# Loading z half as bf16, denser score pairs, w2 turned by DMA and z of batch 1 moved up in a fused attention and max-out kernel

## The chip, the cores and the metric

The kernel runs on one core of one Trainium2 chip. The metric is device time in microseconds (us) of that core. Before the change it was 969.01 us (median of 3 runs, 968.8 to 970.68). The span of a profile is about 2.4 us shorter than the time (966.4 against 968.82 for the same execution).

Names: PE is TensorE, PEld its weight loads, DVE VectorE, ACT ScalarE, POOL GpSimd, SP SyncE. L147 is a line of the kernel; the changed kernel has other line numbers. A "mirror" is a 512 KB block of scores turned by DMA, because the score matrix is symmetric. "Turned" means transposed: zT is z turned, zd the cast copy of z that is turned. A transfer has landed when all its data is there. The tile a_sb holds squared scores, r_sb the relus before them, h_sb the sums copied out of the accumulators at the end of a group (the drain copy). The granted clock is the clock of TensorE in the profile, 1.00 being full; the page is the printed summary of a profile.

## The reference, cut to what matters

```python
def _attn_ref(u, v, z):                       # 8 x 3072 x 256, z 8 x 3072 x 64
    scores = (1.0 / S) * np.matmul(z, z.transpose(0, 2, 1))
    attn = np.maximum(scores, 0.0) ** 2
    return u * np.matmul(attn, v)

def _moe_ref(x, w1, w2, w_out):               # x: 24576 x 256, Dff = 1024
    return np.maximum(x @ w1, x @ w2) @ w_out
```

The kernel uses max(h1, h2) = relu(x(w1-w2)) + x w2, so it needs w15 = w1-w2 and W2o = w2 @ w_out once, and W2o needs w2 transposed (w2T).

## The kernel before

A batch has 24 tiles of 128 rows in 6 groups of 4 tiles. Groups are numbered i over all batches: i = 0 to 5 are batch 0. "Tile n of group g" below is the n-th of the 24 steps of that group. While PE multiplies the squared scores of group i with v, score pairs for later use are put in at chosen slots:

```python
    def pair_slots(i):
        if i == 0:
            return [1, 3] + list(range(6, 40, 4))
        if i == 1:
            return list(range(3, 41, 4))
        ...
    # in score_pair: two products z.zT into PSUM, then
        for h in range(2):
            s, o = s_ps[h][:, lo[h] :], r[:, h, lo[h] :]
            if h == dve_half:                       # VectorE takes one half of every third early pair
                nc.vector.tensor_single_scalar(out=o, in_=s, scalar=0.0, op=ALU.max)
            else:
                nc.scalar.activation(o, s, AF.Relu)
        ...
            nc.vector.tensor_mul(a[:, k : k + 2, :], r, r)
    ...
            early = done < 22                       # dve_half=1 if early and done % 3 == 0
```

The opening loads z of batch 0 in three pieces on SP, v on GpSimd's queue; the third piece is cast on GpSimd:

```python
        z32a = first_z(0, 4)
        z32b = first_z(4, 8)
        z32c = first_z(12, 12)
        ...
        load_v(0, 0, G)
        make_identity(nc, ident)
        for g in range(1, NG):
            load_v(0, g * G, G)
        ...
        on_pool = (nc.gpsimd.tensor_copy, nc.gpsimd.tensor_copy)
        for c in range(0, 12, 4):
            double_first(z32c, 12 + c, 4, at=c, copies=on_pool)
```

In group 2, w2 is turned on PE; at its end W2o is made ahead of the first feed-forward product (ff1, inside ff). All DMA transposes (mirrors, u, z of batch 1) go through the SP queue in program order:

```python
                if i == 2 and n == 16:
                    nc.vector.tensor_sub(w15_sb, w1_sb, w2_sb)
                    for dc in range(KD):
                        tp = mm_psum.tile([P, KF, P], bf16, name="tpw", tag="mm")
                        for j in range(KF):
                            nc.tensor.transpose(tp[:, j, :], w2_sb[:, dc, ts(j, P)], ident)
                        nc.scalar.copy(w2T_sb[:, dc, :, :], tp)
                if b + 1 < B:
                    late = int(b == 0)
                    if (g, n) == (2, 10 if b else 20):
                        load_z(b + 1, 0, NT, held=late)
                    if (g, n) == (3, 4):
                        double_z(b + 1, 0, NT)
                        zT_dma(b + 1)
    ...
            if i == 2:
                for dc in range(KD):
                    ps = mm_psum.tile([P, D], fp32, name="w2o_ps", tag="mm")
                    for nb in range(KF):
                        nc.tensor.matmul(ps, w2T_sb[:, dc, nb, :], w_out_sb[:, nb, :], ...)
                    nc.scalar.copy(W2o_sb[:, dc, :], ps)
            now = waiting if ff_follows(i) else []
            g_sbs = [ff(w) for w in now[:1]]
```

## Time and profile before

| what | value | where it is read |
|---|---|---|
| time, span | 969.01 us, 966.4 us | runs, head of the page |
| PE busy | 99% of the span | busy table |
| PE on the chain that ended last | 96% | chain of waits |
| PE idle in the first 60 us | 60 - 54.97 = 5.0 us | busy time by window |
| PE waits after 60 us | one of 0.2 us | waits of PE by window |

The head, the busy table and the chain's shares, from the page of the kernel before:

```profile
span 966.4 us, 19478 instructions
...
PE 954.8 (99%) x7994; PEld 621.6 (64%) x8042; DVE 487.2 (50%) x847; ACT 557.6 (58%) x1058; POOL 61.0 (6%) x118
...
PE 96%; DVE 1%; issue 1%; ACT 1%; DMA 1%; DVEq 0%; POOLq 0%
```

PE is the limit. So a change can win only where PE waits, or where it does work that can go. This is the view of waits, PE alone, first 60 us, kernel before. Columns: who waited, for whom; us in total, times, longest:

```profile
PE acc_134 L374 <- DVE warm L351: 1.2, 1, 1.2
PE acc_427 L199 <- DVE a_sb L166: 1.1, 3, 0.5
PE acc_427 L199 <- DVE h_sb L214: 0.5, 1, 0.5
PE s_ps L147 <- DVE r_sb L158: 0.5, 1, 0.5
PE acc_134 L199 <- DMA v_sb<-in_v_dram: 0.4, 1, 0.4
PE s_ps L147 <- ACT zT L105: 0.4, 1, 0.4
PE acc_637 L199 <- DVE a_sb L166: 0.4, 1, 0.4
PE tpz L101 <- ACT zd L88: 0.3, 1, 0.3
```

The first is the start and stays. The rest, 3.6 us by these lines, is what the opening had to give. The PE transposes of w2 and the products that read them, from the timeline of PE (start, length):

```profile
46.71 1.07 PE L439 MATMUL tpw<-ident,w_132 128*128 128x128 bf16 x16
...
52.03 1.92 PE L458 MATMUL w2o_ps<-w_out_sb,w2T 128*128 128x256 bf16 x16
```

The transposes are 1.07 us of PE.

### The profile page before, as it was taken

What the parts mean: (1) busy time and instruction counts of PE and PEld (TensorE: products, weight loads), DVE (VectorE), ACT (ScalarE), POOL (GpSimd) and SP (SyncE); (2) the same over time, 40 slices, a digit from 0 to 9 for tenths busy, and PEclk for the clock granted to TensorE, in tenths of its full rate; (3) what the DMA queues carried; (4) which work ended last, traced back from release to release, by engine and by line L of the source; (5) the groups of instructions that cost most, each with busy time, mean ns of one, the idle gap of its engine ahead of it and who ended that gap; (6) DMA issues with size and microseconds to landing.
All of it is one profiled execution on the core that took longest, in us unless ns stands there. A gap on an engine that the chain in (4) does not pass through costs nothing.

```text
span 966.4 us, 19478 instructions
## 1 busy us (share of the span) xinstructions
PE 954.8 (99%) x7994; PEld 621.6 (64%) x8042; DVE 487.2 (50%) x847; ACT 557.6 (58%) x1058; POOL 61.0 (6%) x118
## 2 busy tenths in 40 slices
PE   8999999999999999999999999999999999999998
PEld 4465667675666756667566765676756776566655
DVE  6746454463555534555346553464545554445433
ACT  6757466563575645756456564565556656466433
POOL 3001000100000000000000000000000000000000
PEclk9999999999999999999999999999999999999999
DMA  9999798988689976999869988699967998767611
GB/s 186 186 207 175 135 156 158 179 149 166 134 140 188 146 157 126 164 185 148 150 133 146 184 152 160 131 162 176 150 141 140 157 170 168 135 131 145 124 56 44
DMA packets 382296, 145.99 MB, mean 151 GB/s; under 512 B 360832, under 2 KB 361984, under 8 KB 382208
## 3 DMA queue, kind: packets, MB, share of 16 engines
q1 hardware_dynamic: 365792, 115.25, 62.5%
q0 software_dynamic: 16416, 29.50, 20.8%
q8 instruction: 63, 1.03, 0.4%
q14 instruction: 25, 0.20, 0.1%
HBM read 59.77 MB, written 25.17 MB: 88 GB/s over the span
## 4 chain that ended last, share of the span: by engine, by line
PE 96%; DVE 1%; issue 1%; ACT 1%; DMA 1%; DVEq 0%; POOLq 0%
PE o_ps L263 17%; PE d_ps L234 17%; PE s_ps L147 7%; PE o_ps L255 4%; DMA v_sb<-in_v_dram 1%; DVE a_sb L166 1%; PE acc_12604 L199 1%; PE acc_6354 L199 1%; PE acc_4771 L199 1%; PE acc_3187 L199 1%; PE acc_11103 L199 1%; PE acc_9519 L199 1%; PE acc_7936 L199 1%; PE acc_1582 L199 1%; PE acc_1581 L199 1%
## 5 line engine op out<-in xcount | busy, mean ns | idle before, releaser
L199 PEld LDWEIGHTS <-v_sb 64*128 64x128 bf16 x4608 | 314.6, 94 | 181.4 <-issue 5.9
L160 ACT ACTIVATE r_sb<-s_ps 128x512 bf16<-128x512 f32 (+3 forms) x664 | 333.8, 555 | 90.4 <-PE s_ps L147 88.8
L166 DVE TENSOR_TENSOR a_sb<-r_sb 128x1024 bf16<-128x1024 bf16 x251 | 173.6, 692 | 243.0 <-ACT r_sb L160 239.0
L244 DVE TENSOR_SCALAR g_sb<-d_ps 128x512 bf16<-128x512 f32 x192 | 132.8, 692 | 146.1 <-PE d_ps L234 146.1
L263 PE MATMUL o_ps<-w_out_sb,g_sb 128*128 128x256 bf16 x1536 | 199.1, 273 | 0.0
L234 PE MATMUL d_ps<-xT,w_sb 128*128 128x512 bf16 x720 | 167.4, 379 | 2.6 <-issue 0.2
L263 PEld LDWEIGHTS <-g_sb 128*128 128x128 bf16 x1536 | 150.2, 98 | 20.8
L242 ACT ACTIVATE g_sb<-d_ps 128x512 bf16<-128x512 f32 x192 | 114.8, 598 | 82.0 <-PE d_ps L234 57.1
L147 PE MATMUL s_ps<-zT 64*128 64x512 bf16 (+3 forms) x672 | 148.6, 357 | 0.9 <-DVE r_sb L158 0.5
L270 ACT COPY o_sb<-o_ps 128x512 f32<-128x512 f32 x96 | 56.3, 586 | 150.3 <-PE o_ps L263 149.2
L234 PEld LDWEIGHTS <-w_sb 128*128 128x128 bf16 x768 | 73.2, 98 | 89.6 <-issue 9.8
L255 PE MATMUL o_ps<-W2o_sb,xT 128*128 128x256 bf16 x384 | 73.3, 273 | 0.0
L118 POOL DMA_DIRECT2D un<-in_u_dram x48 | 25.7, 537 | 731.2 <-DMA uT<-un 717.6
L147 PEld LDWEIGHTS <-zT 64*128 64x128 bf16 x672 | 47.6, 94 | 29.0 <-issue 4.6
L220 DVE SCALAR_TENSOR_TENSOR xT<-h_sb,uT 128x512 bf16<-128x512 f32 x96 | 61.8, 685 | 0.0
L164 DVE TENSOR_TENSOR a_sb<-r_sb 128x512 bf16<-128x512 bf16 (+3 forms) x170 | 47.9, 323 | 14.7 <-ACT r_sb L160 14.5
L255 PEld LDWEIGHTS <-xT 128*128 128x128 bf16 x384 | 37.6, 98 | 14.1
L114 POOL DMA_DIRECT2D v_sb<-in_v_dram x48 | 25.8, 546 | 59.1 <-DVE v_sb L113 58.3
L199 PE MATMUL acc_134<-a_sb,v_sb 64*128 64x512 bf16 x24 | 8.7, 377 | 0.5 <-DMA v_sb<-in_v_dram 0.4
L199 PE MATMUL acc_136<-a_sb,v_sb 64*128 64x512 bf16 x24 | 8.7, 378 | 0.0
L199 PE MATMUL acc_137<-a_sb,v_sb 64*128 64x512 bf16 x24 | 8.5, 376 | 0.0
L199 PE MATMUL acc_135<-a_sb,v_sb 64*128 64x512 bf16 x24 | 8.5, 376 | 0.0
(577 smaller groups left out, 1665.3 us busy)
## 6 DMA issues: line engine op xcount, KB each, us to landing
out_dram<-o_sb SPq DMA_DIRECT2D x47, 512.0 KB, 4.0
v_sb<-in_v_dram POOLq DMA_DIRECT2D x48, 256.0 KB, 7.0
un<-in_u_dram POOLq DMA_DIRECT2D x48, 256.0 KB, 5.0
zn<-in_z_dram POOLq DMA_DIRECT2D x7, 384.0 KB, 6.7
a_sb<-a_sb SPq DMA_TRANSPOSE x126, 2.7
at_sb<-a_sb SPq DMA_TRANSPOSE x120, 5.0
uT<-un SPq DMA_TRANSPOSE x48, 3.3
w_132<-in_moe_w_dram POOLq DMA_DIRECT2D x1, 512.0 KB, 5.1
```

What stands on the lines that cost most here:

```text
L147: nc.tensor.matmul(s_ps[h][:, lo[h] :], zT[b][rows, 2 * m + h, :], zT[b][rows, g * G + lo[h] // P : g * G + G, :].rearrange("p t c -> p (t ...
L160: nc.scalar.activation(o, s, AF.Relu)
L164: nc.vector.tensor_mul(a[:, k + h, lo[h] :], o, o)
L166: nc.vector.tensor_mul(a[:, k : k + 2, :], r, r)
L199: nc.tensor.matmul(o, v_sb[b][rows, t, ts(dc, P)], mv, start=first, stop=last)
L220: nc.vector.scalar_tensor_tensor(out=xT[:, dc, :].rearrange("p (t r) -> p t r", r=P), in0=hs[dc].rearrange("p (t r) -> p t r", r=P), scala ...
L234: nc.tensor.matmul(d_ps, w15_sb[:, kc, ts(nb, P)], xT[:, kc, :], start=(kc == 0), stop=(kc == KD - 1),)
L242: nc.scalar.activation(g_sb[:, nb, :], d_ps, AF.Relu)
L244: nc.vector.tensor_single_scalar(out=g_sb[:, nb, :], in_=d_ps, scalar=0.0, op=ALU.max)
L255: nc.tensor.matmul(o_ps[:, t, :], xT[:, dc, ts(t0 + t, P)], W2o_sb[:, dc, :], start=(dc == 0), stop=False,)
L263: nc.tensor.matmul(o_ps[:, t, :], g_sb[:, nb, ts(t0 + t, P)], w_out_sb[:, nb, :], start=False, stop=(nb == KF - 1),)
L270: nc.scalar.copy(o_sb[:, t0 : t0 + 2, :], o_ps)
```

## The change

It removes waits and work from the opening: half of z moves behind the first v tile, so that v lands sooner; score pairs come earlier and VectorE takes fewer relus; w2 is turned by DMA instead of PE; z of batch 1 is loaded and turned earlier; the last two tiles leave one by one. The diff, cut to its core:

```diff
-        for t0 in range(0, G, 2):
-            o_ps = mm_psum.tile([P, 2, D], fp32, name="o_ps", tag="mm")
+        for t0, k in ((0, 2), (2, 1), (3, 1)) if last else ((0, 2), (2, 2)):
+            o_ps = mm_psum.tile([P, k, D], fp32, name="o_ps", tag="mm")
 ... (eviction and store of k tiles instead of 2)
         if i == 0:
-            return [1, 3] + list(range(6, 40, 4))
+            return [1, 3, 6, 9, 12, 15, 18, 21, 25, 29, 33, 37]
         if i == 1:
-            return list(range(3, 41, 4))
+            return list(range(2, 40, 4))
 ...
-            early = done < 22
+            early = done < 18
 ...
-        z32c = first_z(12, 12)
 ...
-        for g in range(1, NG):
+        zn[0] = znat.tile([P, NT, dqk], bf16, name="zn")
+        nc.gpsimd.dma_start(out=zn[0][:, 12:, :], in_=by_tile(z[0])[:, 12:, :])
+        load_v(0, G, G)
+        for g in range(2, NG):
             load_v(0, g * G, G)
 ...
-        on_pool = (nc.gpsimd.tensor_copy, nc.gpsimd.tensor_copy)
-        for c in range(0, 12, 4):
-            double_first(z32c, 12 + c, 4, at=c, copies=on_pool)
+        double_first(zn[0], 12, 4, at=12, copies=[nc.gpsimd.tensor_copy] * 2)
 ...
+                if i == 0 and slot in (4, 12):
+                    both = (nc.gpsimd.tensor_copy, nc.vector.tensor_copy)
+                    lo = 16 if slot == 4 else 20
+                    double_first(zn[0], lo, 4, at=lo, copies=both)
 ...
+                if i == 1 and n == 20:
+                    nc.sync.dma_start_transpose(
+                        w2T_sb.rearrange("p c j r -> p (c j) r"),
+                        w2_sb.rearrange("p c f -> p (c f)"),
+                    )
                 if i == 2 and n == 16:
                     nc.vector.tensor_sub(w15_sb, w1_sb, w2_sb)
-                    for dc in range(KD): ... nc.tensor.transpose(...) ... nc.scalar.copy(...)
                 if b + 1 < B:
                     late = int(b == 0)
-                    if (g, n) == (2, 10 if b else 20):
+                    if (g, n) == (2, 10):
                         load_z(b + 1, 0, NT, held=late)
-                    if (g, n) == (3, 4):
+                    if (g, n) == (3, 4 if b else 0):
                         double_z(b + 1, 0, NT)
                         zT_dma(b + 1)
```

## The prediction

> **What bounds it.** TensorE. The page's busy table gives PE 99% of the 966.4 us span, the chain of waits PE 96%, granted clock 1.000. PE's waits, listed by window, are one of 0.2 us in all after 52 us. So what can be won lies in the opening and the tail. Summed by windows, PE is idle 5.0 us of the first 60, 1.2 of it the start. The waits: first product for v (landed 6.0 us after issue) 0.43; score pair for ACT's zT copy 0.39; zd cast 0.35; first accumulator for VectorE's drain copy 0.54; group 1 (31 to 37 us) for VectorE relus and squares 0.48+0.21+0.55+0.31; before w2o, a square behind the 1.22 us weight subtraction and ACT's w2T copies, 0.38.
>
> **What changes.**
> 1. 384 KB of z leave the queue that competes with the first v tile, so v lands about 1 us earlier or more. The squares (ready about 6.9) then set the first product: gain 0.4 us, 0.6 if the middle z also lands earlier. GpSimd casts fall from 6 (0.55 each) to 4, VectorE gets 2 (about 0.25 each). The Trainium skill, "DMA: Bandwidth & Descriptors", section "SWDGE vs HWDGE vs iDMA", says that a cast during DMA goes from GpSimd only; so this load stands ahead of the later v tiles, which have slack in the trace.
> 2. Denser pairs put pair 6 two slots after the zT transposes instead of four. ACT must first do seven relus at about 0.54 and the 1.02 us copy, and one cast stands behind a square on VectorE. Waits there should grow to about 1 us and eat step 1's 0.4; in exchange one score pair more is done when group 0 ends.
> 3. VectorE relu only for the first 18 pairs removes two 0.68 us relus exactly at the group 1 waits; with one pair of lead (1.08 us of PE) the 1.55 us nearly vanishes: gain 1.4. No pair stands at the end of group 0, so the 0.54 drain wait goes: gain 0.5.
> 4. w2 by DMA: 16 PE transposes leave (1.07 us, timeline), with ACT's 1.93 us of copies and most of the 0.38 wait: gain 1.4. But it becomes the third 512 KB transpose on an SP queue where those before it took 6.4 and 3.2 us to issue, and landing takes 4.3 to 10.4. Estimated landing 48 us, its reader now at 49 to 50: a wait of 0 to 2 us, mean 0.4.
> 5. Tail: the last eviction halves (0.59 to 0.37 us), as does the last store (its data moved for 0.7 us): gain 0.5.
> 6. z of batch 1 earlier: PE never waited for it, gain 0.
>
> Sum: about 0.2+1.4+0.5+1.4+0.5-0.4 = 3.6 us, all on PE's chain: from 969.0 to 965.4 us, range 963.6 to 967.9. Chances: faster 0.005, within 2% 0.985, slower 0.01.
>
> **Right or wrong in the profile.** First product at about 6.8 us (was 7.3); a PE wait for zd or zT between 10 and 12.5; none for h_sb at the first group boundary; under 0.3 us for a_sb and r_sb in group 1; no tpw lines; w2o at 48.5 to 49.5 (was 52.0); 0.5 us less after the last matmul.
>
> **What would make it wrong.** The bf16 z landing after 9 us: VectorE is in order, its cast would block squares. The w2T transpose landing late. ACT, 1.09 us per pair against PE's 1.08, limiting group 1. The run spread (968.8 to 970.7) is half the gain.

## The result, and the profile after

The changed kernel took 971.1 us (median of 5, 970.23 to 974.93), the kernel before 968.8 us in the same rounds. The ratio is 1.0026, 95% interval 1.0004 to 1.0048: slightly slower, where 3.6 us faster was predicted. Here and below a ratio is the mean time of one kernel's fast runs over that of the other's of the same rounds, so it is not quite the ratio of the medians quoted. All runs quoted here counted as fast.

The head, the busy table and the chain's shares, page of the changed kernel:

```profile
span 968.7 us, 19445 instructions
...
PE 955.2 (99%) x7978; PEld 623.1 (64%) x8026; DVE 485.5 (50%) x847; ACT 556.8 (57%) x1059; POOL 60.6 (6%) x117
...
PE 96%; DMA 2%; DVE 1%; ACT 1%; issue 0%; SPq 0%
```

PE's busy total hardly moved and its share is still 99%. These averages do not show the fault; only the DMA share of the chain rose. The waits of PE in the first 70 us of the changed kernel do show it:

```profile
PE w2o_ps L461 <- DMA w2T<-w: 4.4, 1, 4.4
PE acc L377 <- DVE warm L351: 1.2, 1, 1.2
PE s_ps L147 <- ACT zT L105: 0.6, 1, 0.6
PE acc L199 <- DVE h_sb L214: 0.4, 1, 0.4
PE s_ps L147 <- DVE zT L105: 0.3, 1, 0.3
```

All waits of PE for squares, for VectorE's relu and for v are gone: the opening worked. One new wait of 4.42 us stands above it. The w2o products were free to start at 53.55 - 4.42 = 49.1 us instead of 52.03, so 2.9 us had been won by then. They started at 53.55. The view of the tile w2T, changed kernel (for the products: nanoseconds min/median/max of one):

```profile
...
L461 PE MATMUL w2o_ps<-w_out_sb,w2T x16: 283/421/422, 53.6 to 56.7; 128*128 128x256 bf16 x16
L440 SPq DMA_TRANSPOSE w2T<-w x1: 6248/6248/6248, 45.2 to 45.2; - x1
...
  PE w2o_ps L461: 4.4, 1
...
DMA to landing us min/median/max: 8.4/8.4/8.4
```

The transpose was issued at 45.15 us and landed 8.4 us later. And the products that had waited took 421 ns each, where they took 272 before. The busy time by windows, below, tells why. The timeline of PE has it in one line (start, length, the wait before it):

```profile
53.55 3.46 PE L461 MATMUL w2o_ps<-w_out_sb,w2T 128*128 128x256 bf16 x16 [4.42 <-DMA w2T<-w]
```

Columns of the windows: window, its length, busy us (instructions) of PE, PEld, DVE, ACT, POOL, then the granted clock, the DMA share and GB/s:

```profile
49.00:50.00 1.00, 0.13 (x2) 0.00 (x0) 0.32 (x1) 0.00 (x0) 0.00 (x0) 1.00 0.97 158
...
53.00:54.00 1.00, 0.45 (x3) 0.33 (x4) 0.00 (x0) 0.00 (x0) 0.00 (x0) 0.66 1.13 214
54.00:55.00 1.00, 1.00 (x6) 0.72 (x5) 0.00 (x0) 0.00 (x0) 0.00 (x0) 0.50 1.12 201
...
56.00:57.00 1.00, 1.00 (x7) 0.69 (x6) 0.00 (x0) 0.00 (x0) 0.00 (x0) 0.63 1.17 218
57.00:58.00 1.00, 0.95 (x6) 0.46 (x5) 0.09 (x1) 0.89 (x2) 0.00 (x0) 1.00 1.12 209
```

After the idle the granted clock is 0.50, back to 1.00 by 57 us. So w2o took 3.46 us instead of 1.92. The wait and the half clock together cost 4.42 + 1.54 = 6.0 us, more than everything the change won.

The tail, by contrast, went as planned. The last piece of the chain (start, length), kernel before and then changed kernel:

```profile
962.45 0.59 ACT o_sb L270
```

```profile
965.29 0.37 ACT o_sb L271
```

From its start to the end of the span it was 966.4 - 962.45 = 3.95 us, and is 968.7 - 965.29 = 3.41 us.

### The profile page after: what moved, and what is told of

Its sections match the earlier page's. It is cut to its first block, busy times and chain, and to the rows that moved or that the text cites. A ratio compares the mean times of both kernels' runs of the same rounds, so it can differ in the third digit from the quotient of the medians.

```text
span 968.7 us, 19445 instructions
## 1 busy us (share of the span) xinstructions
PE 955.2 (99%) x7978; PEld 623.1 (64%) x8026; DVE 485.5 (50%) x847; ACT 556.8 (57%) x1059; POOL 60.6 (6%) x117
## 4 chain that ended last, share of the span: by engine, by line
PE 96%; DMA 2%; DVE 1%; ACT 1%; issue 0%; SPq 0%
PE acc L199 49%; PE o_ps L264 17%; PE d_ps L234 17%; PE s_ps L147 7%; PE o_ps L256 4%; DMA at_sb<-a_sb 1%; DMA w2T<-w 1%; ACT r_sb L160 0%; PE w2o_ps L461 0%; PE acc L377 0%; DVE a_sb L166 0%; ACT zT L105 0%; PE tpz L101 0%; DVE h_sb L417 0%; DVE r_sb L158 0%
## 5 line engine op out<-in xcount | busy, mean ns | idle before, releaser
L160 ACT ACTIVATE r_sb<-s_ps 128x512 bf16<-128x512 f32 (+3 forms) x666 | 334.6, 555 | 88.7 <-PE s_ps L147 86.9
L199 PE MATMUL acc<-a_sb,v_sb 64*128 64x512 bf16 x2688 | 340.9, 376 | 0.1
L199 PE MATMUL acc<-at_sb,v_sb 64*128 64x512 bf16 x1920 | 238.0, 376 | 0.7 <-DVE h_sb L214 0.4
L271 ACT COPY o_sb<-o_ps 128x512 f32<-128x512 f32 (+1 forms) x97 | 56.3, 581 | 150.0 <-PE o_ps L264 148.9
L205 ACT COPY h_sb<-acc 128x512 f32<-128x512 f32 x92 | 51.5, 589 | 76.2 <-PE acc L199 76.2
L207 DVE TENSOR_TENSOR h_sb<-h_sb,acc 128x512 f32<-128x512 f32 x92 | 61.1, 685 | 64.1 <-ACT h_sb L205 64.1
```

The source lines that it names most:

```text
L199: nc.tensor.matmul(o, v_sb[b][rows, t, ts(dc, P)], mv, start=first, stop=last)
L207: nc.vector.tensor_add(hs[dc], hs[dc], acc[0, dc])
L271: nc.scalar.copy(o_sb[:, t0 : t0 + k, :], o_ps)
```

## The experiments

Theory A: the whole loss is the wait of w2o for the w2T transpose and the half clock after it; the rest of the change wins what was predicted. Its rivals: B, the other parts cost something too; C, the transpose is late because the z load of batch 1 was moved into the same stretch; D, the DMA queue is full for so long that an extra transpose is paid for wherever it stands. C and D say why A's wait is so long. The kernel before gave medians of 969.29, 969.03, 968.94 and 968.88 us. Times (us), ratio to before and interval:

| run | edit | median (range) | ratio, 95% interval |
|---|---|---|---|
| changed kernel | | 971.1 (970.23 to 974.93) | 1.0026 [1.0004, 1.0048] |
| e_pe | changed, w2 on PE | 966.28 (965.56 to 966.88) | 0.9964 [0.9951, 0.9977] |
| e_early | changed, w2T queued earlier | 973.1 (966.49 to 975.12) | 1.0022 [0.9997, 1.0047] |
| e_zlate | changed, z load and turn late | 974.24 (970.93 to 980.98) | 1.0052 [1.0024, 1.008] |
| e_dummy | changed, PE kept busy in the wait | 969.74 (968.87 to 972.88) | 1.0003 [0.9985, 1.0021] |
| p_w2dma | before, w2 by DMA | 968.89 (967.69 to 971.51) | 0.9992 [0.9972, 1.0013] |
| e_pe_spare | e_pe and an unread transpose | 966.91 (965.86 to 967.21) | 0.9967 [0.9948, 0.9986] |
| e_deadline | changed, queue in order of need | 967.23 (965.02 to 970.05) | 0.9973 [0.9947, 0.9999] |
| p_pairs | before, denser pairs | 966.42 (966.22 to 970.25) | 0.9971 [0.9949, 0.9992] |
| e_zmid | changed, z load late only | 969.74 (966.35 to 972.31) | 1.0002 [0.998, 1.0023] |
| e_w2o_after_ff1 | changed, reader later | 968.77 (966.59 to 969.76) | 0.9989 [0.9975, 1.0003] |
| e_zmid_ff1 | both | 967.93 (966.86 to 973.4) | 0.9996 [0.9976, 1.0017] |
| p_zload | before, opening load | 968.45 (967.9 to 977.63) | 1.0018 [0.9986, 1.0049] |
| e_pe_zmid | e_pe, z load late | 966.04 (965.74 to 972.4) | 0.9981 [0.9962, 0.9999] |
| e_pe_zlate | e_pe, z load and turn late | 965.75 (965.61 to 966.05) | 0.9968 [0.9956, 0.998] |
| e_pe_oldload | e_pe, old opening load | 965.92 (965.8 to 966.62) | 0.9971 [0.9958, 0.9984] |
| p_tail | before, tail only | 967.94 (967.36 to 968.87) | 0.999 [0.9978, 1.0002] |

All gave correct results. Ranges are those of the fast runs listed with each kernel, five or six.

### e_pe: w2 turned on PE again

```diff
-                if i == 1 and n == 20:
-                    nc.sync.dma_start_transpose(w2T_sb..., w2_sb...)
                 if i == 2 and n == 16:
                     nc.vector.tensor_sub(w15_sb, w1_sb, w2_sb)
+                    (the PE transposes and ACT copies of the kernel before)
```

> The changed kernel with w2 turned on TensorE again, all else as changed. Theory A (the loss is the 4.42 us wait of w2o for the w2T transpose plus the half clock after it, 3.46 us for w2o where it was 1.92): both go, 1.1 us of transposes and up to 0.4 of a wait for squares come back, so 971.1 - 6.0 + 1.3 = about 966.4 us, faster than before by about 2.4. Rival B (the denser pairs or the moved z loads cost what the trace of the one run does not show): stays above 968.8.

Measured 966.28 us, within 0.2 us of theory A and below before by more than the interval. Its w2o started at 49.50 us at full clock, and no wait of PE stands in its trace after 60 us:

```profile
49.50 1.92 PE L463 MATMUL w2o_ps<-w_out_sb,w2T 128*128 128x256 bf16 x16
```

B falls: what is left of the change wins about what was predicted for it, and the DMA transpose of w2 turned a gain of 0.36% into a loss of 0.26%.

### e_dummy: PE kept busy during the wait

```diff
                     ps = mm_psum.tile([P, D], fp32, name="w2o_ps", tag="mm")
+                    for _ in range(40 if dc == 0 else 0):
+                        nc.tensor.matmul(ps, warm[:, :P], warm[:, :D], start=True, stop=True)
```

> The changed kernel with 40 products of 128x256 on a constant tile before w2o (about 4.4 us of work in place of the 4.42 us of idle; the results are overwritten). Theory A: the half clock (0.50 in the records from 53.6 to 56.7 us) comes from the idle; kept busy, the clock stays at 1.00, w2o takes 1.9 us, and the time falls by 1.5 us to about 969.6 although the wait itself is no shorter. Rival: the slow w2o comes from the DMA traffic at that time or is read wrongly; then nothing changes, about 971.

Measured 969.74 us; the span fell from 968.7 to 967.3. The windows of this run:

```profile
53.00:54.00 1.00, 1.00 (x11) 0.89 (x10) 0.00 (x0) 0.00 (x0) 0.00 (x0) 1.00 1.13 213
54.00:55.00 1.00, 1.00 (x12) 0.89 (x11) 0.00 (x0) 0.24 (x1) 0.00 (x0) 1.00 1.14 208
```

The DMA share is the same as in the changed kernel (1.13, 1.14 against 1.13, 1.12), the clock is 1.00, and the products took 272 ns (median). So the half clock came from the idle, not from the DMA traffic, and it is worth about 1.4 us. The Trainium skill, "TensorE: Matmul & The Clock Gate", section "What's actually happening", says that PE falls to half rate after an idle window of about 3.4 us; here the wait was 4.42 us, and the half rate lasted 3.4 us (53.3 to 56.7 us, read from windows of 0.2 us of the changed kernel).

### e_early: the transpose six tiles sooner

```diff
-                if i == 1 and n == 20:
+                if i == 1 and n == 14:
                     nc.sync.dma_start_transpose(w2T_sb..., w2_sb...)
```

> The changed kernel with the w2T transpose queued at tile 14 of group 1 instead of tile 20, so ahead of two mirror transposes on the SP queue. Theory A with the queue place as the reason for lateness: issued at about 34.5 us instead of 45.2, landed by about 43, no wait of w2o, clock 1.00 throughout, about 965.1 us. If the transpose were late because of what stands before it on the data side (w2 itself landing late), w2o would still wait and the time stay near 971.

The transpose was issued at 33.7 us, landed 9.6 us later, and w2o found it there at 48.6 us: that half of the expectation held. The time did not: 973.1 us, from 966.49 to 975.12. Waits of PE after 80 us in its profiled run (969.94 us, one of the faster ones):

```profile
PE s_ps L147 <- DMA zT<-zd: 3.8, 2, 2.3
PE acc L199 <- DMA at_sb<-a_sb: 0.9, 1, 0.9
```

Two transposes that stand behind it were late instead: first zT of batch 1, then a mirror. This is what D says. In the changed kernel they stand behind it too, but there PE had already lost 6.0 us and did not wait for them. The four runs above 972 us have a mean granted clock of 0.996, the profiled one 1.000, so this profile does not show all that they lost.

### e_zlate: z of batch 1 at its old places

```diff
-                    if (g, n) == (2, 10):
+                    if (g, n) == (2, 10 if b else 20):
                         load_z(b + 1, 0, NT, held=late)
-                    if (g, n) == (3, 4 if b else 0):
+                    if (g, n) == (3, 4):
```

> The changed kernel with z of batch 1 loaded and turned at its old places (tile 20 of group 2, tile 4 of group 3). Rival theory C: the transpose took 8.4 us from issue to landing because the 384 KB of z were loaded (44.3 us) into the same stretch; then it lands about 2 to 3 us sooner, the wait falls to about 2 us, and the time to about 968.5. Theory A (its place third on the queue, with mirrors taking the engines anyway): lands within 1 us of before, time 970 to 971.

w2T landed in 4.3 us instead of 8.4 and w2o had no wait worth naming (0.4 us for its first weights): C holds for the late landing, even more than expected. But the time rose to 974.24 us. Waits of PE after 60 us:

```profile
PE s_ps L147 <- DMA zT<-zd: 4.6, 1, 4.6
```

Its granted clock was again 0.50 after this idle. So with the extra transpose on the queue z could not stay at both its late places, and its move was itself what delayed that transpose. This profile (972.82 us) is one of the faster runs; those of 975 to 981 us, at a mean clock of 0.993 to 0.995, were not profiled.

### p_w2dma: the DMA transpose alone, on the kernel before

Edit: on the kernel before, the PE transposes and copies are taken out and the transpose at tile 20 of group 1 is put in, as in the diff of the change.

> The kernel before with one part of the change: w2 turned by DMA at tile 20 of group 1, z of batch 1 left at its old late place. Theory D (the DMA engines are full from 25 to 100 us, so one more 512 KB transpose is paid by whichever transfer has the next deadline): w2o finds w2T in time (landing about 49 us, as 4.3 us did in the run with the late z), but the transpose of z for batch 1 lands too late and the score pairs of batch 1 wait 3 to 5 us: time 970 to 974, slower than before. Rival C (only the collision of w2T with the moved z load costs): no wait anywhere, 969 - 1.4 = 967.6 us.

Median 968.89 us, between the two expectations: no loss, but not the 1.4 us that PE no longer spent either. The transpose landed in 5.0 us and w2o did not wait: it started at 51.4 us (52.0 before), although the first product came 0.37 us later than before. In the profiled run (its slowest, 971.51) PE then waited 3.6 us for a mirror, until 90.8 us, and not for zT. D holds in kind, not in place or size. The median is 1.3 us above the 967.6 expected without a wait; what the faster runs waited for was not profiled.

### e_zmid: only the load of z back

```diff
-                    if (g, n) == (2, 10):
+                    if (g, n) == (2, 10 if b else 20):
```

> The changed kernel with only the load of z for batch 1 put back to tile 20 of group 2; its cast and transpose stay at the changed, earlier place (tile 0 of group 3). The two runs before told two things apart only together: with load and transpose both late, the transpose of w2 landed in 4.3 us instead of 8.4, but zT came 4.6 us too late. If the collision of the two loads is the cause of the 4.42 us wait: w2T lands in 4 to 6 us, w2o waits under 0.6 us at full clock, and zT is queued at about 72 us with a wait of 0 to 2 us: 965.3 to 967.5 us. If the collision was chance: w2T lands after 8 us again and the time is 970 or more.

Timelines of the SP queue and of GpSimd, changed kernel, around the transpose (start, and time to issue):

```profile
36.03 9.02 SPq L181 DMA_TRANSPOSE at_sb<-a_sb  x2
45.15 6.25 SPq L440 DMA_TRANSPOSE w2T<-w  x1
```

```profile
44.28 0.53 POOL L75 DMA_DIRECT2D zn<-in_z_dram  x1 [10.95 <-DVE zn L74]
44.80 0.54 POOL L118 DMA_DIRECT2D un<-in_u_dram  x1
```

And the same two of e_zmid:

```profile
34.69 9.28 SPq L181 DMA_TRANSPOSE at_sb<-a_sb  x2
44.07 2.52 SPq L440 DMA_TRANSPOSE w2T<-w  x1
```

```profile
49.01 0.54 POOL L75 DMA_DIRECT2D zn<-in_z_dram  x1 [15.98 <-DVE zn L74]
49.53 0.54 POOL L118 DMA_DIRECT2D un<-in_u_dram  x1
```

The two transposes before it together took 9.0 us to issue in one and 9.3 us in the other, so the place in the queue is the same. With the 384 KB of z and the 256 KB of u queued just before it, w2T took 6.25 us to issue and 8.4 to land; without them 2.52 and 4.5:

```profile
DMA to landing us min/median/max: 4.5/4.5/4.5
```

The load of u moved along because it stands behind z in the order of GpSimd, so the share of each is not told apart. Every run that has the transpose at tile 20 and the early load agrees (8.1 to 9.5 us: e_dummy 8.2, e_w2o_after_ff1 8.1, e_pe_spare 9.5), every run with the late load too (4.3 to 5.0). C is settled: the collision is the larger part of the wait (0.6 us of it stayed in e_zmid, as a wait for the first weights). The Trainium skill, "DMA: Bandwidth & Descriptors", section "Issuing engines are not separate DMA queues", says that transfers of all issuing engines run on the same 16 DMA engines and interleave. The trace agrees: loads issued by GpSimd more than doubled the 2.52 us that a transpose on SP took to issue.

The time, however, came in two levels: 966.35, 966.45, 967.92 and 971.55, 971.71, 972.31 us. The profiled run is the fastest, and even it has this wait of PE after 60 us:

```profile
PE acc L199 <- DMA at_sb<-a_sb: 1.5, 1, 1.5
```

The three high runs were not profiled, but their mean granted clock is 0.996 to 0.998, against 1.000 in the three low ones and 0.998 in the profiled run of the changed kernel with its one stretch of half clock. So a stretch of half clock is likely in them; which transfer was late is not shown.

### e_w2o_after_ff1 and e_zmid_ff1: the reader later

```diff
-            if i == 2: (w2o products)
             now = waiting if ff_follows(i) else []
             g_sbs = [ff(w) for w in now[:1]]
+            if i == 2: (w2o products)
```

> The changed kernel with the w2o products put after the first ff1 (which does not need them), so 3.4 us later in TensorE's order; all transfers as changed. If the wait is nothing but the late landing (53.5 us against a reader at 49.1): the reader is ready at 52.5, waits about 1 us, and after so short an idle the clock should stay higher: 971.1 - 3.4 - 0.8 to 1.5 = 966.2 to 966.9 us, with perhaps up to 1 us of it given to a new wait for zT or a mirror. If the transfers only follow the reader (a queue that fills up with TensorE's progress), the wait stays near 4 us and so does the time.

> Both of the two edits above together. Expected: no wait of w2o at all, no half clock; 965.0 to 966.5 us unless zT or a mirror is waited for. This is the candidate for a version that beats both kernels with the DMA transpose kept; to beat the version with w2 turned on TensorE (966.3) it must stay under 966.

In e_w2o_after_ff1 w2T landed at 44.4 + 8.1 = 52.5 us and the reader started at 52.49 with hardly a wait (0.6 us for its first weights, none that the view lists for PE), so the queue did not merely follow the reader. The time fell less than expected, to 968.77 us: PE then waited 0.35 us for the copy of W2o, which the edit had moved closer to its use, and 2.1 us for a mirror, until 87.3 us, and the clock was 0.50 after that. e_zmid_ff1, with both edits, had no wait for w2T, and a median of 967.93 us with single runs up to 973.4 (that one profiled: waits of 2.6 us for a mirror and 2.2 us for zT). Neither beats e_pe.

### e_pe_spare: the same transpose, read by nobody

```diff
+                if i == 1 and n == 20:
+                    spare = tpool.tile([P, KD, KF, P], bf16, name="spare", tag="at_sb")
+                    nc.sync.dma_start_transpose(spare..., w2_sb...)
                 (w2T made on PE as in e_pe)
```

> The changed kernel with w2 turned on TensorE, and still the same DMA transpose of w2 at the same place, into a spare tile that nobody reads. Theory D: even without a reader it delays the transfers behind it, so waits for zT or for mirrored blocks of 1 to 4 us appear after 60 us and the time is 967.5 to 970 (against 966.3 without it). Rival (only the dependency of w2o on the transpose costs): 966.3, no new wait.

966.91 us against 966.28, in different calls; the ratios to before are 0.9967 and 0.9964. The expectation of D was too high. (The spare tile also takes one of the 13 buffers of the mirrors; the run does not separate that from the transfer.) Only a wait of 0.44 us for a mirror appeared, ending at 86.1 us. Set beside e_zmid, whose only late wait was 1.52 us and ended at 85.8 us: the difference, 1.08 us, is the 1.07 us of PE transposes that e_zmid saves. e_pe, without the extra transpose, reached the same product at about 85 us and did not wait. In these two runs the mirror came at about 86 us whatever PE did before, so what PE wins by leaving the transposes to the DMA it gives back there. In the other profiled runs with the extra transpose that waited for a mirror after 60 us it came at 86.9 to 90.8 us. So D is best put like this: with the extra 512 KB on the queue, PE can meet a late mirror at 86 us or after. This is a reading of single profiles; no run tests it by itself.

### e_deadline: transfers in the order in which they are needed

Edit: w2T at tile 14 of group 1; z of batch 1 loaded at tile 2 and turned at tile 18 of group 2; the mirrors of block 5 (needed last) held back until tile 20.

> The changed kernel with its transfers put in order of deadline: w2T queued at tile 14 of group 1, z of batch 1 loaded at tile 2 of group 2 and its transpose queued at tile 18, the mirrors of block 5 held back behind it. Theory D with slack to spend (the engines are at 0.3 to 0.8 busy from 100 to 115 us): no wait of w2o, zT or mirrors, time about 965, a little under the 966.3 with w2 turned on TensorE. If the total load and not the order is what binds, some wait of 1 to 4 us remains and the time is 967 to 970.

Three runs at 965.02 to 966.02, three at 968.43 to 970.05. In the profiled run (968.43, the fastest of the upper three) w2T took 15.4 us to land, with waits of 0.5 us for w2T, 1.4 us for VectorE's g_sb and 1.4 us for zT. The 965 of the good runs is the lowest time seen, but the kernel does not hold it.

### p_pairs, p_zload, p_tail: the other parts alone

Edits: on the kernel before, only the slots and `early = done < 18`; only the opening's loads and casts; only the tail (each as in the diff of the change).

> The kernel before with the denser score pairs and the VectorE relu for 18 pairs only, nothing else. My prediction put 1.4 us (group 1) and 0.5 us (drain) on this part: about 967.1. If the opening load is needed for it (zT not ready for pair 6, so the wait of about 1 us comes without the earlier v): about 968.

> The kernel before with only the opening's loads and casts changed (12 tiles of z as bf16 behind the first v, casts on GpSimd and VectorE). My prediction gave step 1 a gain of 0.4 to 0.6 us: v no longer waited for, first product at about 6.7 instead of 7.3 us, time 968.4 to 968.8 against 969.0 to 969.3 of before. If the opening is bound by ACT's evacuations (the copy of zT ready at about 12.8 us in either kernel) the gain at the start is gone by the score pair that waits for zT: time as before, within 0.2.

> The kernel before with only the last two tiles evicted and stored one by one. My prediction: the time from the last product to the end falls by 0.5 us (4.0 us before), so 968.4 to 968.6 us against 968.9 to 969.1 of before.

p_pairs: 966.42 us, a gain of 2.6 us, more than the 1.9 expected. It is nearly the whole gain of e_pe (3.0). Its trace has no wait for squares before w2o either. p_tail: 967.94 us, a gain of 0.9 by the medians and 0.1% by the ratio, with an interval that includes no gain; the chain's 0.54 us is the better measure. p_zload: four runs at 967.9 to 968.67 and two at 975.23 and 977.63. The slow one was profiled. Waits of PE in its first 60 us:

```profile
PE acc L199 <- DMA at_sb<-a_sb: 7.1, 1, 7.1
...
```

A mirror came 7.1 us late there, and the clock was 0.50 from 47 to 52 us. The other high run was not profiled. Why this mirror is late in some executions was not found.

### e_pe_zmid, e_pe_zlate, e_pe_oldload: what e_pe needs

Edits: to e_pe, the z load of batch 1 late as in e_zmid; load and transpose late as in e_zlate; the old opening load.

> The changed kernel with w2 turned on TensorE and the load of z for batch 1 at tile 20 of group 2 (old place), its transpose at tile 0 of group 3 (changed place). If the extra DMA transpose of w2 made the mirrors late in the run that differs from this one only in it, this one runs at one level, 966 to 966.9 us, with no wait after 60 us. If the late load alone does it, two levels (966.4 and 971) are seen again.

> The same with the transpose of z back at tile 4 of group 3 too, so without step 6 of the change at all. My prediction said the move of z is worth nothing by itself, since TensorE never waited for zT before: 966 to 967 us. If TensorE, now 3 us earlier, has used up the slack, a wait for zT of 1 to 5 us appears and the time is 967 to 971.

> The changed kernel with w2 turned on TensorE and the opening load and casts as before the change. Measures step 1: my prediction gave it 0.4 us at the first product, most of it lost again at the zT copy. So 966.3 to 966.8 us against 966.3, with a wait for v of about 0.7 us back in the trace. If step 1 carries more, 967 or above.

e_pe_zlate took 965.75 us, all five listed runs within 0.44 us, the steadiest of all. PE, now 3 us earlier, still does not wait for zT. e_zlate differs from it only in how w2 is turned, and took 974.24 us: the 4.6 us wait for zT there came from the extra transpose. So with w2 on PE the move of z is worth nothing. With w2 on the DMA its two halves differ: the earlier turn is needed (e_zlate waits for zT, the profiled e_zmid does not), and the earlier load is what delays w2T. e_pe_zmid had five runs at 965.74 to 966.33 and one at 972.4; e_zmid had three of six at the high level. Too few to say that the extra transpose makes the high level more frequent, and since no high run of either was profiled, what happens in one stays open. e_pe_oldload: 965.92 us, with a wait for v of 0.8 us back in the trace and no loss of time that shows. The new opening load is worth nothing measurable.

## Why the prediction was wrong

- **Step 4, the step that failed** ("a wait of 0 to 2 us, mean 0.4"). The mechanism was named: third on the SP queue, landing close to its reader. The reader was placed right (49 to 50 us predicted, 49.1 measured); the landing was not (48 predicted, 53.5 measured). The wait was 4.42 us, eleven times the term in the sum. Two causes were left out. First, I costed the transpose near the low end of its range of 4.3 to 10.4 us, as if step 6 did not exist: issued at 45.15 us as measured, even 4.3 us would have landed it at 49.5, not at 48. Step 6 put 384 KB of z, and with it 256 KB of u, beside it, which made the landing 8.4 us (e_zmid: 4.5 us without). Second, I gave idle time no price beyond itself; the half clock added 1.54 us (e_dummy). With 4.42 + 1.54 in place of 0.4, the predicted 965.4 becomes 971.0; measured 971.1. That this fits to 0.1 us is partly luck: by w2o the change had won 2.9 us, where steps 1 to 4 had forecast 3.5.
- **Step 6** ("gain 0"): right that z by itself wins nothing (e_pe_zlate), wrong to stop there. A move that wins nothing can still cost, when it lands on another new transfer.
- **Step 4's gain of 1.4 us** was not to be had either. Where w2o's wait is cured, PE waits for a mirror at 86 to 87 us (e_zmid, e_w2o_after_ff1), and p_w2dma shows no gain. Also, the 0.38 us wait before w2o that this step counted went with step 3 (p_pairs), while p_w2dma kept 0.22 us of it.
- **Step 3** (gain 1.4 and 0.5): right. The waits for squares and VectorE's relu in group 1 are gone; the wait for VectorE's drain copy at the first boundary is gone, but 0.43 us of it comes at the next one (36.55 us), which I did not foresee. p_pairs measured 2.6 us for the whole part.
- **Step 1**: the first product came at 6.67 us (predicted 6.8, before 7.32). The cast during DMA did run from GpSimd, landed 5.2 us after issue, and no later v tile was waited for, as the prediction had it with the skill. As predicted the early start did not last; e_pe_oldload shows no loss without it. The cast of bf16 on GpSimd took 0.57 us apiece (2.29 for four), no less than from fp32 (0.55).
- **Step 2**: the wait for zT grew from 0.39 to 0.56 us, not to 1 us; a wait of 0.31 us for VectorE's zT copy came before it, at 7.4 us, which was not foreseen.
- **Step 5**: 0.54 us by the chain, 0.5 predicted.
- **ACT as a new limit in group 1**: did not happen; PE has no wait for ACT's relus there.

## What to carry to other kernels

Before moving work from the busiest engine to a DMA queue, list what that queue carries between issue and deadline, from all issuing engines and including the other lines of the same change: here 1.07 us of PE work was exchanged for a transfer whose landing went from 4.5 to 8.4 us with the loads of z and u beside it. Price a wait of PE with the half clock that can follow it: here it added 1.5 us to one of 4.4 us, and it followed waits as short as 2.1 us. And try the parts of a change alone: here three lines (the slots of two groups and the limit of 18 for the relus) were nearly all of the gain, and leaving w2 on PE made 971.1 into 966.3 us.

## What the Trainium skill lacked or had wrong

- "TensorE: Matmul & The Clock Gate", section "What's actually happening", gives an idle window of about 3.4 us, running freely, for the fall to half rate. Waits of 4.42, 4.63 and 7.12 us were followed by a granted clock of 0.50, as it says; but so were waits of 2.10 us (e_w2o_after_ff1) and 2.62 us (e_zmid_ff1), while one of 3.59 us (p_w2dma) left it at 1.00. Read in windows of 0.2 us, the half clock lasted 3.4 us each time (6.8 us in p_zload), which fits the page's window. But in the two short cases PE had been idle for only 2.1 us of the 3.4 us before the fall, and in e_w2o_after_ff1 the clock fell at 88.1 us, 0.8 us after PE had resumed. So the window need not be idle throughout. The 3.59 us may have been shared by two windows.
- "DMA: Bandwidth & Descriptors" says that transfers share the engines, in the section named above, and has an effective bandwidth for DMA transposes, but gives no landing time of one under load. The same 512 KB transpose from SBUF to SBUF, queued at tile 20, landed in 4.3 to 5.0 us with the late load of z, and in 8.1 to 9.5 us with 384 KB of z and 256 KB of u queued just before it. Queued at tile 14, 1.0 to 2.4 us behind 512 KB of w_out and 256 KB of u, it landed in 9.6 us (e_early), and in 15.4 us where z followed as well (e_deadline).
- I found no page that says of a kernel on one core that it can run at two levels: e_zmid 966.4 and 971.6 us, p_zload 968 and 975 to 978 us. Of these high runs one was profiled, that of 977.63 us, and it shows a mirror 7.1 us late. The kernel before is not free of it: 3 of its 44 runs beside the experiments took 973 us at a mean clock of 0.998.
